# Threshold attention and hash-routed experts on one core: PSUM tiles at the seam, and the order of gathers and weight loads

## The chip, the core and the metric

The kernel runs on one NeuronCore of a Trainium2 chip. The metric is the time of one execution on the device in microseconds (us), lower is better; the median of several runs counts. Five engines work side by side, each with its own instruction queue, and wait for each other through semaphores: PE (TensorE, with weight loads shown as PEld), DVE (VectorE), ACT (ScalarE), POOL (GpSimd) and SP (SyncE, which here only issues transfers).

## The reference, cut to what matters

Attention over 8 batches of 8 heads (576 queries, 64 wide) keeps only scores within `tau` of the row's maximum. Its output is seen as 4608 rows of 512, and each row goes to one of 8 experts by a hash of its token id:

```python
scores = scale * np.matmul(q, k.transpose(0, 1, 3, 2))
thresh = np.max(scores, axis=-1, keepdims=True) - tau
scores = np.where(scores >= thresh, scores, -1000000000.0)
...
attn = attn / (np.sum(attn, axis=-1, keepdims=True) + 1e-09)
out = np.matmul(attn, v)
...
expert_idx = token_ids * np.int64(2654435761) % np.int64(E)
for e in range(E):
    xe = x[mask]
    h = np.maximum(xe @ w1[e], 0.0)
    out[mask] = h @ w2[e]
```

`w1[e]` is 512 x 1024 and `w2[e]` is 1024 x 512, all in fp32. A weight load is 2 MB.

## The kernel before

The attention half walks over 32 pairs of heads in 5 steps each, in an order written out by hand (`tc.manual_schedule()`): queues execute instructions as the source emits them. Scores are made in PSUM tiles `sc` of the pool `ps_sc` (two tiles of two banks each, line 87). [...]

The experts' half runs over the experts e = 0 to 7 in an order sorted by load. Each expert has two layers, and each layer is computed with seven products in place of eight (a Strassen scheme, function `seven`, line 930): sums and differences of blocks of weights and inputs are made on VectorE (`left` and `right`, line 862 for subtractions, line 865 for additions), PE multiplies them (line 945), and the results are added up from PSUM on VectorE. `layer1` runs `seven` twice for each expert (a product of layer 2 is 16 matmul rows in the trace, one of layer 1 is 8), `layer2` once. After each of a product's results, `seven` calls back a "side" function with a step number 0 to 5; side work of other experts is emitted there: `side1` in layer 1, `side2` in layer 2.

At the seam, expert 0's first layer has been started while attention was still running (`early_h`, line 641: three quarters of the contraction, blocks fo 0 to 7). `late_h` (line 661) adds the last quarter. It takes the blocks in the order 0, 6, 1, 7, 2, 3, 4, 5; blocks 6 and 7 were held open in `ps_sc`'s two tiles, blocks 2 and 4 use these two tiles next, and blocks 0, 1, 3 and 5 use the pool `ps_x`, which has one tile. For all but 6 and 7 VectorE adds the PSUM tile to h (line 672) and ScalarE applies the relu (line 673). Then `ps_sc` is closed (line 1079) and a pool `ps_m` of four tiles opens over the same PSUM (line 1080); `bank2` (line 858) hands out its tiles for all products that follow.

The work of an expert that matters here:

- `fetch(e)` (line 1048) gathers expert e's rows of x into the five tiles `xg` by five indirect DMAs on POOL's queue (line 122). For e = 1 each has a small copy ahead of it (line 1052) that makes it wait for a relu of `late_h`.
- `turn_x(e)` (line 1055): VectorE transposes the five tiles into `xq` (line 1059), then SP issues 16 DMAs, the moves, that lay them out as `xT` (line 1067).
- `load_w1` and `load_w2` (lines 135 and 141) load weights on SP's queue (DMAs of lines 137 and 143) into pools of two tiles; each reads the expert's number into a register first (line 132). `load_w1(e + 2)` must wait for expert e's layer 1.
- `sums_w1(e + 1)` and `sums_x(e + 1)` are emitted two at a time in steps 1 to 5 of layer 2 of expert e; the sums over x need the moves.
- `put_squares` transposes results on VectorE (line 1031) and scatters them with indirect DMAs on POOL's queue (line 1039).

For expert 0 all of `turn_x(1)` runs in step 0 of layer 2. For the later experts it runs within layer 1 of the expert before.

Of the kernel before, what the change touches and what calls it, by code (L numbers as in the profile page):

```python
# [9 lines left out]
FP32 = mybir.dt.float32  # L10
# [6 lines left out]
PSUM = bass.MemoryType.PSUM  # L17
# [3 lines left out]
def kernel(  # L21
# [16 lines left out]
    E, _, F = w1.shape  # L38
    P = 128
# [43 lines left out]

    consts = ctx.enter_context(tc.tile_pool(name="consts", bufs=1))
    w_pool = ctx.enter_context(tc.tile_pool(name="w_pool", bufs=2))
    sc_stack = ctx.enter_context(ExitStack())
    ps_sc = sc_stack.enter_context(tc.tile_pool(name="ps_sc", bufs=2, space=PSUM))

    ident = consts.tile([P, P], FP32, name="ident")
    u128 = consts.tile([P, P], BF16, name="u128")  # L90
# [30 lines left out]
    def gather(src, dst, idx):  # L121
        nc.gpsimd.indirect_dma_start(  # L122
            out=dst, out_offset=None, in_=src,
            in_offset=bass.IndirectOffsetOnAxis(ap=idx, axis=0),
            bounds_check=src.shape[0] - 1, oob_is_err=False)
# [4 lines left out]
    def expert_at(e):  # L130

        return nc.values_load(order_i[0:1, e:e + 1], engines=[mybir.EngineType.SP],
                              min_val=0, max_val=E - 1)

    def load_w1(e):
        w1_sb = w_pool.tile([P, CO, F], FP32, name="w1_sb")
        nc.sync.dma_start(out=w1_sb[:],
                          in_=w1[bass.ds(expert_at(e), 1)].rearrange("o (c p) f -> p (o c) f", p=P))
        w_tiles[e, 1] = w1_sb
# [7 lines left out]
    with tc.tile_pool(name="a_q", bufs=1) as a_q, \  # L147
# [513 lines left out]
        def late_h(new_tile):  # L661

            w1_sb = w_tiles.pop((0, 1))
            for fo in LATE:
                h_ps = held.pop(fo) if fo in held else new_tile(fo)
                for i in range(2):
                    nc.tensor.matmul(h_ps[:, i, 0:CH0], lhsT=w1_sb[:, CO - 1, fo * P:fo * P + P],
                                     rhs=xT_0[:, CO - 1, i * CH0:i * CH0 + CH0],
                                     start=(fo < FO - 2), stop=True)
                h3 = h_0[:, fo, 0:caps[0]].rearrange("p (i t) -> p i t", i=2)  # L670
                if fo < FO - 2:
                    nc.vector.tensor_tensor(out=h3, in0=h3, in1=h_ps[:, :, 0:CH0], op=ALU.add)
                    nc.scalar.activation(h3, h3, AF.Relu)
                else:
                    nc.scalar.activation(h3, h_ps[:, :, 0:CH0], AF.Relu)
# [17 lines left out]
        def fill(n):  # L693
            for _ in range(n):
                next(h_pieces, None)
# [140 lines left out]
    with tc.tile_pool(name="m_x", bufs=1) as m_x, \  # L836
# [18 lines left out]
        halves = [m_s.tile([P, 2, CH], FP32, name=n) for n in ("p1", "u2", "u3", "u4")]  # L855
        CHL = 32 * (NB - 4) // 2

        def bank2():
            return ps_m[0].tile([P, 2, 512], FP32, name="bank2")

        def sub(out, in0, in1):
            return lambda: nc.vector.tensor_tensor(out=out, in0=in0, in1=in1, op=ALU.subtract)  # L862
# [47 lines left out]
        def sums_w1(e):  # L910
            return left(*w1_blocks(w_tiles[e, 1]), triple(w1_s, 0, C2))

        def sums_w2(e):
            s1 = None
            if e == E - 1:
                spare = w_pool.tile([P, CO, F], FP32, name="w1_sb")
                s1 = w_tiles["s1"] = spare[:, :, 0:D2]
            return left(*w2_blocks(e, w_tiles[e, 2]), w2_sums(e), s1)

        def sums_x(e):  # L920
            return right(*x_blocks(e), triple(x_s, 0, C2, caps[e] // 2))

        def sums_h(e, c0, c1):
            return right(*h_blocks(c0, c1, half2(e)), triple(h_s, c0, c1, half2(e)))

        def run(work, n=1):
            for _ in range(min(n, len(work))):
                work.pop(0)()
# [38 lines left out]
        def layer1(e, side):  # L967

            w, half = w_tiles.pop((e, 1)), caps[e] // 2
            for g in range(NG):  # L970
                outs = [h_0[:, FH * i + 2 * g:FH * i + 2 * g + 2, half * k:half * k + half]
                        for i in range(2) for k in range(2)]
                seven(w1_blocks(w), triple(w1_s, 0, C2), x_blocks(e), triple(x_s, 0, C2, half), 2 * P * g,
                      outs, True, lambda step: side(g, step))

        def layer2(e, side):

            w, half = w_tiles[e, 2], half2(e)
            outs = [oT[:, C2 * i:C2 * i + C2, half * k:half * k + half]
                    for i in range(2) for k in range(2)]  # L980
            a = w2_blocks(e, w)
            if e == E - 1:
                a[2] = w_tiles["s1"]
            seven(a, w2_sums(e), h_blocks(0, FH, half),
                  triple(h_s, 0, FH, half), 0, outs, False, side)
# [42 lines left out]
        def put_squares(e, i):  # L1028

            s0, s1 = ((0, NH), (NH, -(-caps[e] // 32)))[i]  # L1030
            nc.vector.transpose(  # L1031
                out=o_q[i][:, 0:s1 - s0].rearrange("p n a c -> p c n a"),
                in_=oT[:, :, 32 * s0:32 * s1].rearrange("p c (n q) -> p c n q", q=32))
            for s in range(s0, s1):
                put_rows(o_q[i][:, s - s0].rearrange("p a c -> p (a c)"), qidx[:, e, s:s + 1],
                         rows=out_q)
# [11 lines left out]
        def fetch(e):  # L1048
            for k in range(KT):
                if e == 1:  # L1050

                    nc.gpsimd.tensor_copy(mark[0:1, :], h_0[0:1, k, 0:1])
                gather(x_dram, xg_bufs[k][:], gidx_x[:, e, k:k + 1])

        def turn_x(e):


            def squares(k):
                return lambda: nc.vector.transpose(
                    out=xq[:, :, 32 * k:32 * k + 32],  # L1060
                    in_=xg_bufs[k][:].rearrange("p (d a) -> p d a", a=32))

            def move():
                for g in range(4):
                    s0, s1 = 32 * KT * g, min(32 * KT * (g + 1), caps[e])
                    for r in range(4):
                        nc.sync.dma_start(out=xT_bufs[e % 2][32 * r:32 * r + 32, :, s0:s1],  # L1067
                                          in_=xq[32 * g:32 * g + 32, r::4, 0:s1 - s0])

            return [squares(k) for k in range(KT)] + [move]  # L1070

        with tc.tile_pool(name="ps_x", bufs=1, space=PSUM) as ps_x, tc.manual_schedule():
            run(sums_w2(0), 4)
            fill(18)
            late_h(lambda fo: (ps_sc.tile([P, 2, 512], FP32, name="sc") if fo in (2, 4) else
                               ps_x.tile([P, 2, 512], FP32, name="xT_ps")))
            fetch(1)
            run(sums_h(0, 0, FH), 4)
        sc_stack.close()
        ps_m = [ctx.enter_context(tc.tile_pool(name="ps_m", bufs=4, space=PSUM))]  # L1080

        with tc.manual_schedule():
            for e in range(E):
                more = e + 1 < E
                turns = turn_x(e + 1) if more else []

                if e > 0:
                    w2_work, h_work = sums_w2(e), sums_h(e, 0, 2)

                    def side1(g, step):  # L1090
                        if g == 0:
                            run(w2_work)
                            if step == 0:
                                put_squares(e - 1, 1)
                        else:
                            run(h_work)
                        if step > 2:
                            run(turns, 1 if g == 0 else 2)

                    layer1(e, side1)  # L1100
                    run(sums_h(e, 2, FH), 4)
                if e + 2 < E:
                    load_w1(e + 2)
                x_work = (sums_w1(e + 1) + sums_x(e + 1)) if more else []

                def side2(step):
                    if step == 0:
                        run(turns, len(turns))
                        if e + 2 < E:
                            fetch(e + 2)  # L1110
                    else:
                        run(x_work, 2)
                    if more and step == 3:
                        put_squares(e, 0)
                    if not more and step == 4:
                        put_out(e, (0,))

                layer2(e, side2)
                run(x_work, len(x_work))
                if e + 2 < E:  # L1120
                    load_w2(e + 2)


            def middle():
                put_out(E - 1, (1, 2), (3,))

            last_tile(middle)
# [74 lines left out]
```

## Time and profile before

| what | value |
|---|---|
| median of 3 runs | 922.66 us (922.28 to 922.70) |
| the profiled execution | 933.93 us |
| span of its trace | 932.2 us |
| granted TensorE clock, mean | 0.998 |
| bytes moved by DMA | 113.11 MB, mean 121 GB/s |
| PE, stage 0 to 528 us | 517.94 us busy |
| PE, stage 900 to 933 us | 25.12 us busy |

The profiled execution is 1.2% longer than the median of the plain runs. Its span leaves out 1.7 us around the program. Times within it are counted from the start of the span. In a line of the timeline the columns are start, length, engine, source line, operation, output and inputs by the program's names, shape, and the count of merged instructions; brackets hold the idle time of the engine before it and what ended that. SPq lines are DMAs that SyncE issues; their length is the time of issuing, not of the transfer.

### The profile page before, as it was taken

The numbers are of one execution on the slowest core, as the hardware profiler recorded it, in microseconds if no ns is written. First come the engines' busy times: TensorE is split into PE (matmuls) and PEld (weight loads), VectorE is DVE, ScalarE is ACT, GpSimd is POOL, SyncE is SP. The second block draws the span as 40 slices with busy tenths as digits, with TensorE's granted clock in tenths as the row PEclk, the third lists the DMA queues.
The fourth block names the chain that finished last, engine by engine and source line by source line (L and its number), as shares of the span: only waits on it lengthen the run. The fifth ranks groups of instructions, "written<-read, shape, count | busy, mean of one in ns | idle before, by whom it ended". The sixth has DMA issues, their size and how long they took to land.

```text
span 932.2 us, 20728 instructions
## 1 busy us (share of the span) xinstructions
PE 911.4 (98%) x7495; PEld 662.9 (71%) x7495; DVE 759.5 (81%) x1658; ACT 458.3 (49%) x741; POOL 408.1 (44%) x522
## 2 busy tenths in 40 slices
PE   7999999999999999999999998999999999999996
PEld 4666666666666666665667877888887978879785
DVE  7999999999999999999854685867867686786741
ACT  6888888888888889888702010110202112020210
POOL 4233332436666653465323371643717164350712
PEclk9999999999999999999999999999999999999999
DMA  7355454463555666852113616355352734511101
GB/s 179 88 146 124 107 147 108 120 151 92 115 129 168 151 172 178 211 127 64 32 25 140 191 54 186 126 124 192 93 173 100 196 127 121 200 43 44 46 8 54
DMA packets 114807, 113.11 MB, mean 121 GB/s; under 512 B 32456, under 2 KB 89318, under 8 KB 114704
## 3 DMA queue, kind: packets, MB, share of 16 engines
q1 hardware_dynamic: 105168, 92.64, 37.2%
q0 software_dynamic: 9104, 18.91, 7.2%
q8 instruction: 61, 1.00, 0.4%
q14 instruction: 42, 0.34, 0.1%
q10 hardware_dynamic: 432, 0.21, 0.1%
HBM read 81.99 MB, written 21.50 MB: 111 GB/s over the span
## 4 chain that ended last, share of the span: by engine, by line
PE 62%; issue 21%; POOL 8%; DVE 3%; DMA 2%; ACT 2%; another core or an unknown queue 1%; SPq 1%; POOLq 0%; DVEq 0%; ACTq 0%
PE av L316 18%; PE sc L238 15%; PE bank L945 13%; PE tr L285 11%; POOL out_dram L1039 6%; PE sc L649 3%; PE av L285 1%; POOL xg L122 1%; DMA xT<-xq 1%; ACT w L263 1%; DMA xg<-x_scratch,gidx_x 1%; DMA k_sb<-in_k_dram 1%; ACT wT_b L306 1%; SPq L1067 0%
## 5 line engine op out<-in xcount | busy, mean ns | idle before, releaser
L263 ACT ACTIVATE w<-ns,nmx 128x576 f32<-128x576 f32 x288 | 220.4, 777 | 28.5 <-DVE ns L249 28.2
L1039 POOL DMA_INDIRECT out_dram<-o_q,qidx x128 | 141.0, 1102 | 194.8 <-DVE o_q L1031 133.8
L274 DVE SCALAR_TENSOR_TENSOR w<-ns,thr,w 128x576 f32<-128x576 f32 x288 | 226.2, 817 | 0.0
L249 DVE TENSOR_SCALAR_CACHE_REDUCE ns<-sc 128x576 f32<-128x576 f32 x288 | 205.7, 747 | 7.6 <-PE sc L238 6.6
L256 POOL TENSOR_SCALAR thr<-nmx,drop 128x2 f32<-128x2 f32 (+1 forms) x160 | 104.5, 653 | 186.7 <-DVE ns L249 174.1
L238 PE MATMUL sc<-k_sb,q 64*128 64x288 f32 (+1 forms) x1280 | 178.6, 423 | 0.9 <-DVE ns L249 0.5
L285 PEld LDWEIGHTS tr<-ident,w 64*128 64x128 f32 x2624 | 106.1, 138 | 94.6 <-ACT wT_b L306 32.7
L285 PE MATMUL tr<-ident,w 64*128 64x64 f32 x2624 | 139.0, 230 | 6.1 <-ACT wT_b L306 2.8
L952 ACT ACTIVATE h<-h 128x576 f32<-128x576 f32 (+1 forms) x56 | 38.8, 693 | 158.8 <-DVE h L865 127.8
L238 PEld LDWEIGHTS sc<-k_sb,q 64*128 64x128 f32 (+1 forms) x1280 | 92.8, 177 | 23.2 <-DVE ns L249 8.5
L955 ACT COPY p<-bank 128x576 f32<-128x576 f32 (+2 forms) x22 | 14.0, 635 | 183.4 <-PE bank L945 157.9
L316 PE MATMUL av<-wT_a,v 128*64 128x320 f32 (+1 forms) x704 | 100.4, 418 | 0.4 <-DVE xm L355 0.3
L945 PE MATMUL bank<-h,w_sb 128*128 128x288 f32 (+2 forms) x384 | 95.6, 405 | 2.3 <-issue 1.5
L945 PEld LDWEIGHTS bank<-h,w_sb 128*128 128x128 f32 x384 | 92.5, 294 | 4.2 <-issue 1.9
L306 ACT COPY wT_a<-tr 128x512 f32<-128x512 f32 (+1 forms) x128 | 81.7, 638 | 20.7 <-PE tr L285 20.2
L306 ACT COPY wT_b<-tr 128x512 f32<-128x512 f32 (+1 forms) x128 | 81.4, 636 | 15.3 <-PE tr L285 8.6
L945 PE MATMUL bank<-xT,w_sb 128*128 128x288 f32 (+1 forms) x336 | 87.5, 410 | 0.0
L316 PE MATMUL av<-wT_b,v 128*64 128x256 f32 x640 | 83.2, 389 | 0.0
L945 PEld LDWEIGHTS bank<-xT,w_sb 128*128 128x128 f32 x336 | 63.8, 190 | 19.0
L945 PE MATMUL bank<-h_s,w_s 128*128 128x288 f32 (+2 forms) x256 | 63.0, 404 | 1.9 <-DVE h_s L862 1.9
L316 PEld LDWEIGHTS av<-wT_a,v 128*64 128x64 f32 x704 | 43.7, 136 | 29.2 <-DVE xm L355 0.8
L945 PEld LDWEIGHTS bank<-h_s,w_s 128*128 128x128 f32 x256 | 50.0, 195 | 13.3 <-DVE h_s L862 2.3
(168 smaller groups left out, 1117.7 us busy)
## 6 DMA issues: line engine op xcount, KB each, us to landing
w_sb<-in_moe_w_dram SPq DMA_DIRECT2D x16, 2048.0 KB
q<-in_q_dram SPq DMA_DIRECT2D x62, 288.0 KB
v<-in_v_dram SPq DMA_DIRECT2D x32, 256.0 KB
x_scratch<-xm SPq DMA_DIRECT2D x32, 256.0 KB
xT<-xq SPq DMA_DIRECT2D x84, 80.0 KB
k_sb<-in_k_dram SPq DMA_DIRECT2D x31, 144.0 KB
k_sb<-in_k_dram SPq DMA_DIRECT2D x32, 112.0 KB
x_scratch<-xg SPq DMA_DIRECT2D x9, 256.0 KB
```

What stands on the lines that cost most here:

```text
L238: nc.tensor.matmul(sc[out_rows, i, 0:S2], lhsT=q_sb[rows, h, q0:q1], rhs=k_sb[rows, h], start=True, stop=True)
L249: nc.vector.tensor_scalar(out=ns[:].rearrange("p (i s) -> p i s", i=2), in0=sc[:, :, 0:S2], scalar1=-1.0, scalar2=None, op0=ALU.mult, op1= ...
L256: nc.gpsimd.tensor_scalar(out=thr[:, 0:j + 1], in0=stats[n][0][:, 0:j + 1], scalar1=drop[:], scalar2=None, op0=ALU.add)
L263: nc.scalar.activation(w, nss[n, j][:], AF.Exp, bias=stats[n][0][:, j:j + 1], scale=-1.0)
L274: nc.vector.scalar_tensor_tensor(out=w, in0=nss.pop((n, j))[:], scalar=stats[n][1][:, j:j + 1], in1=w, op0=ALU.is_le, op1=ALU.mult, accum_ ...
L285: nc.tensor.transpose(dst[:, r, 64 * c:64 * c + 64], src[rows, c0:c0 + P], ident[rows, rows])
L306: nc.scalar.copy(dst, tr[:, :, 0:64 * n_c].rearrange("p r (c q) -> p r c q", c=n_c))
L316: nc.tensor.matmul(av[64 * j:64 * j + 64, g, c0:c1], lhsT=v_sb[:, c, 64 * j:64 * j + 64], rhs=wT[g][:, i, c0:c1], start=(c == 0), stop=stop)
L649: nc.tensor.matmul(h_ps[:, i, 0:CH0], lhsT=w1_sb[:, co, fo * P:fo * P + P], rhs=xT_0[:, co, i * CH0:i * CH0 + CH0], start=(co == 0), stop= ...
L945: nc.tensor.matmul(ps[:, i, 0:width], lhsT=lhsT, rhs=y[:, c], start=c == 0, stop=c == n_k - 1)
L952: nc.scalar.activation(c, c, AF.Relu)
L1039: inst = nc.gpsimd.indirect_dma_start(out=rows[:, :], out_offset=bass.IndirectOffsetOnAxis(ap=idx, axis=0), in_=o_sb, in_offset=None, boun ...
```

## The change

`ps_sc` stays open to the end. The pools `ps_x` and the four-tile `ps_m` give way to one `ps_m` of two tiles, opened before `late_h`, which takes from it what it took from `ps_x`. `bank2` hands out tiles of the two pools in turn. In `side2`, `fetch(e + 2)` moves from step 0 to step 2, and `load_w1(e + 2)` from ahead of layer 2 to step 4.

```diff
-    sc_stack = ctx.enter_context(ExitStack())
-    ps_sc = sc_stack.enter_context(tc.tile_pool(name="ps_sc", bufs=2, space=PSUM))
+    ps_sc = ctx.enter_context(tc.tile_pool(name="ps_sc", bufs=2, space=PSUM))
...
+        ps_m = ctx.enter_context(tc.tile_pool(name="ps_m", bufs=2, space=PSUM))
+        turn = [0]
+
         def bank2():
-            return ps_m[0].tile([P, 2, 512], FP32, name="bank2")
+            turn[0] ^= 1
+            if turn[0]:
+                return ps_sc.tile([P, 2, 512], FP32, name="sc")
+            return ps_m.tile([P, 2, 512], FP32, name="bank2")
...
-        with tc.tile_pool(name="ps_x", bufs=1, space=PSUM) as ps_x, tc.manual_schedule():
+        with tc.manual_schedule():
             run(sums_w2(0), 4)
             fill(18)
             late_h(lambda fo: (ps_sc.tile([P, 2, 512], FP32, name="sc") if fo in (2, 4) else
-                               ps_x.tile([P, 2, 512], FP32, name="xT_ps")))
+                               ps_m.tile([P, 2, 512], FP32, name="bank2")))
             fetch(1)
             run(sums_h(0, 0, FH), 4)
-        sc_stack.close()
-        ps_m = [ctx.enter_context(tc.tile_pool(name="ps_m", bufs=4, space=PSUM))]
...
-                if e + 2 < E:
-                    load_w1(e + 2)
                 x_work = (sums_w1(e + 1) + sums_x(e + 1)) if more else []
 
                 def side2(step):
                     if step == 0:
                         run(turns, len(turns))
-                        if e + 2 < E:
-                            fetch(e + 2)
                     else:
                         run(x_work, 2)
+                    if step == 2 and e + 2 < E:
+                        fetch(e + 2)
+                    if step == 4 and e + 2 < E:
+                        load_w1(e + 2)
```

## The prediction

> **What bounds the kernel now.** I read the page first, then busy time by stage, then the instructions in order of time around the seam between attention and experts, then SyncE's queue. The page says who the bound is:
>
> ```profile
> span 932.2 us, 20728 instructions
> ...
> PE 911.4 (98%) x7495; PEld 662.9 (71%) x7495; DVE 759.5 (81%) x1658; ACT 458.3 (49%) x741; POOL 408.1 (44%) x522
> ```
>
> TensorE is busy for 98% of the span, so only its gaps can be won. Busy time by stage, for the experts' half (columns: stage length; busy of PE, PEld, DVE, ACT, POOL; clock; DMA share; GB/s):
>
> ```profile
> 528.00:545.00 17.00, 16.64 (x70) 12.80 (x69) 16.02 (x17) 2.01 (x3) 9.65 (x9) 1.00 0.45 155
> 545.00:575.00 30.00, 26.68 (x108) 22.14 (x107) 17.68 (x27) 5.16 (x8) 15.24 (x15) 1.00 0.54 148
> 575.00:600.00 25.00, 25.00 (x104) 21.41 (x103) 19.58 (x21) 1.32 (x2) 10.76 (x10) 1.00 0.39 135
> ...
> 640.00:900.00 260.00, 260.00 (x1056) 216.28 (x1055) 187.88 (x225) 36.93 (x55) 117.11 (x107) 1.00 0.38 113
> ```
>
> From 575 to 900 PE never stops. So whatever PE gains before 575 reaches the end undiminished, and buffers or loads cannot give anything later. Gaps exist at three places: the seam, one at 534, one near 565 to 571. The seam in order of time (start, length, engine, line; the idle time before it in brackets):
>
> ```profile
> 493.78 1.13 PE L667 MATMUL xT_ps<-xT,w_sb 128*128 128x288 f32 x4
> 494.75 1.13 PE L667 MATMUL sc<-xT,w_sb 128*128 128x288 f32 x4
> 495.82 0.78 PEld L667 LDWEIGHTS xT_ps<-xT,w_sb 128*128 128x128 f32 x4 [0.40 <-DVE h L672]
> ...
> 500.82 1.24 PE L667 MATMUL xT_ps<-xT,w_sb 128*128 128x288 f32 x4
> ...
> 502.10 0.75 DVE L672 TENSOR_TENSOR h<-h,xT_ps 128x576 f32<-128x576 f32 x1 [0.36 <-PE xT_ps L667]
> ...
> 502.90 8.15 PE L945 MATMUL bank<-h,w_sb 128*128 128x288 f32 x32 [0.84 <-DVE h L672]
> 503.60 1.36 DVE L862 TENSOR_TENSOR h_s<-h 128x1152 f32<-128x1152 f32 x1 [0.75 <-ACT h L673]
> ...
> 511.84 3.07 DVE L1059 STREAM_TRANSPOSE xq<-xg 128x512 f32<-128x512 f32 x5
> ...
> 616.51 7.92 PE L945 MATMUL bank<-h,w_sb 128*128 128x288 f32 x32
> ```
>
> The last line is the same product pair two experts on, for comparison. The reader is to see two things. late_h's blocks on the single xT_ps tile wait for VectorE's add of the block before. And expert 0's first product (502.90) waits for the last of these adds (502.10 + 0.75 = 502.85), although it reads only h blocks 0 to 3: the sum over block 5 is none of its operands. It is the pools that make this wait, ps_m's four tiles opening over ps_sc and ps_x only when both are free. SyncE's queue at the same place, and the next gap:
>
> ```profile
> 502.09 0.39 SPq L137 DMA_DIRECT2D w_sb<-in_moe_w_dram  x1
> 514.97 12.52 SPq L1067 DMA_DIRECT2D xT<-xq  x16
> 528.35 0.41 SPq L143 DMA_DIRECT2D w_sb<-in_moe_w_dram  x1
> ...
> 528.91 0.76 DVE L862 TENSOR_TENSOR x_s<-xT 128x576 f32<-128x576 f32 x1 [5.42 <-DMA xT<-xq]
> ...
> 534.70 4.12 PE L945 MATMUL bank<-x_s,w_s 128*128 128x288 f32 x16 [0.36 <-DVE x_s L862]
> ```
>
> The 16 moves that turn x for expert 1 land at 528.9; VectorE waits 5.42 us for them, and PE for its sums: the 16 rows from 530.29 should end at 534.17, the next start at 534.70, a gap of 0.5 us.
>
> [...] In this trace the w2 load issued at 528.35 follows the moves and they still land by 528.9. [...] In this trace PE is full from 575 to 900 with loads of 2 MB in flight.
>
> **The change part by part.**
>
> *late_h on two tiles.* No instruction is added. An unhindered block of four rows takes 494.75 - 493.78 = 0.97 us. Eight blocks from 493.78 end at 493.78 + 8 x 0.97 = 501.54. Blocks 1, 3, 5 now wait for the add two turns earlier (0, 1), done by 497.85: no wait. Blocks 2 and 4 still wait for ScalarE's relu of the held blocks 6 and 7, which by the same timeline end at 497.02 and 499.11; their turns come at 493.78 + 4 x 0.97 = 497.66 and 493.78 + 6 x 0.97 = 499.60. Covered, by 0.5 us.
>
> *First product.* Its bank is now that of block 2, whose add ends at 499.04 + 0.75 = 499.79. It reads blocks 0 to 3; the relu of block 3 ends at 500.80 + 0.68 = 501.48. So it starts at 501.54 instead of 502.90: 1.36 us. Its 32 rows took 8.15 us against 7.92 at 616.51, because the row after the wait comes late: 0.23 us. Sum 1.59 us.
>
> *What is late next.* Product 2 starts at 501.54 + 3.88 = 505.42 (16 rows, 3.88 us apart by the products at 632.03 and 635.91) and reads block 5, whose relu ended at 503.56. Product 3 needs the third of the h_s sums: it ended at 507.74, and comes about 0.3 us earlier as block 5 ends at 501.54 instead of 501.82; needed at 509.30. Slack 1.9 us, before 3.1. Not late. Bounds for this part: the waits gone cannot give more than all idle of PE at the seam, 1.6 us; if the product met another wait of the same pools it would be the add of block 5 again, about 0.3 us earlier than now: 0.3 us gained. I take 1.59.
>
> *The rotation of banks.* bank2 alternates ps_sc and ps_m, two tiles each: still four in turn. Each product of the experts waits for the same instruction as before, by the built order of both kernels. Cost 0.
>
> *Gathers two products later.* In GpSimd's queue nothing stands between the old place and the new one, and each gather waits, as before, for the VectorE transpose that read its xg tile. All five issue where they did. The words of the change describe the source, not the queue. Cost 0; cover is not needed.
>
> *w1 loads four products later.* For experts 3 to 7 SyncE's queue has the same order as before (the moves were issued in layer 1 already), so nothing moves. For expert 2's w1 the DMA and its expert number (a register load and three small instructions) go past the 16 moves: from 502.09 to behind them, before w2's load. First use: the sums at 574.71, which wait for it. Two loads now run together after about 527; 4 MB, at the 385 GB/s that the slice at 532 shows for one, take about 11 us, so about 540, doubled for caution 550. Cover 25 us. What leaves 502 to 511 is the load that ran beside expert 1's gathers; their transposes (511.84) showed no idle time, so nothing is won there. What joins 527 to 540 is beside GpSimd's scatters, which stand 1.3 to 1.5 us apart under a load (534.25, 535.73, 537.01) and 1.3 without one (546.45, 547.74). Cost 0, bounds -0.5 (the gap at 534 goes) to +0.3 (the last moves are touched).
>
> *The end.* put_out's two tiles wait for copies long done. 0.
>
> The moves start when the five transposes are done, and these follow the first oT add, which follows product 2. So the moves, their landing and the gap at 534 all come 1.59 us earlier, and PE keeps what it won. The profiled execution took 933.93 us (span 932.2); it becomes 932.3. The median of the runs is 922.66, 1.2% lower; the waits are engine latencies, which I don't scale: 922.66 - 1.6 = 921.1 us, -0.17%. (0.2%, about what a measurement can tell from no change, is 1.85 us here.)
>
> **The rivals.**
>
> *More than the seam* (919): the DMA side changes with the load gone from the gathers' time, and the gap at 534 (0.5) and part of the stall near 565 to 571 go. The stage 545 to 575 lacks 30.00 - 26.68 = 3.3 us of PE. Half of that and 0.5 beyond the seam's 1.6: 922.66 - 1.6 - 0.5 - 1.6 = 919.0. For: the stall lies where moves and gathers crowd the DMA engines. Against: no weight load lies there, before or after.
>
> *Taken back at 534* (922.7): the moves land at the old time, because their own transfers set it, and PE waits 1.6 us longer. For: that wait is live, so nothing buffers it. Against: the moves' start is tied to product 2.
>
> *Slower* (929): the w1 load, issued right behind the 16th move, gets on the DMA engines before the last moves have landed. The live wait for x_s passes each microsecond on to PE. The load took from 502.09 to about 511, over 8 us; all of it ahead of the moves gives 922.66 - 1.6 + 8 = 929.1. It decides from a delay of 1.6 + 1.85 = 3.45 us. Against: the w2 load already stood at that place, 0.86 us behind the last move (514.97 + 12.52 = 527.49 to 528.35), and did no harm.
>
> *It doesn't do what it says* holds for the gathers and for all w1 loads but one, and is in the sum.
>
> **How the numbers follow.** Seam alone 0.60, more 0.20, taken back 0.08, slower 0.12. Around 1.6 us the seam alone falls beyond 1.85 us in somewhat under half its cases (0.27), because the waits in timed runs may be a little longer and the small gap at 534 may shrink. Faster 0.27 + 0.20 = 0.47; same 0.33 + 0.08 = 0.41; slower 0.12. The time is 921.1. The range, 918.4 to 923.0, leaves out the slower case and the far end of "more".
>
> **What would show it.** Right: L667's blocks 0.97 us apart without idle; the first L950 row at about 501.5 in the changed kernel, its 32 rows in 7.9 us; x_s still waiting some 5 us for xT; the w1 load at about 527, just ahead of w2's; gathers right after the transposes; PE full after 575. Wrong: a wait for VectorE at the first product; x_s's wait grown by over a microsecond; idle PE at the sums of w1 near 574; a different gap near 565 that outweighs the seam.

## The result, and the profile after

| | median | range | executions |
|---|---|---|---|
| before, beside it on the same chip | 922.62 us | 921.77 to 923.83 | 22 |
| after | 921.12 us | 920.38 to 922.09 | 22 |

The ratio is 0.9984, with a 95% interval of 0.9978 to 0.9990: 1.5 us faster (0.9 to 2.0 by the interval). That is clear of zero in these 22 executions of each, but below the 0.2% (1.85 us) that the prediction took as the least that counts as faster. The predicted time was 921.1 us.

The page of the kernel after:

```profile
span 919.5 us, 20728 instructions
...
PE 906.9 (99%) x7495; PEld 662.5 (72%) x7495; DVE 758.2 (82%) x1658; ACT 457.6 (50%) x741; POOL 408.9 (44%) x522
```

Its span is 12.7 us below the one shown of before, and the medians are 1.5 us apart. So most of what these two profiles differ by is not the change. The waits of PE show it. Each line has what PE was to compute and the line of the source, what it waited for, and then us in total, the number of waits and the longest; "issue" is a wait for nothing that the profile shows. Before:

```profile
PE tr L285 <- ACT wT_b L306: 2.8, 4, 1.7
...
PE bank L945 <- DVE h_s L862: 1.9, 1, 1.9
...
PE bank L945 <- issue: 1.5, 2, 1.0
PE bank L945 <- DVE h L672: 0.8, 1, 0.8
...
PE bank L945 <- DVE x_s L862: 0.4, 1, 0.4
```

After, the whole view:

```profile
PE tr L284 <- ACT wT_a L305: 2.0, 3, 0.7
PE tr L701 <- POOL ident masks.py:199: 1.6, 1, 1.6
PE av L315 <- DVE xm L354: 0.3, 1, 0.3
PE sc L237 <- DVE drop L712: 0.3, 1, 0.3
PE av L284 <- ACT oT L331: 0.2, 1, 0.2
PE sc L237 <- DVE ns L248: 0.2, 1, 0.2
```

No wait of the experts' products (L945 before, L950 after) is left. Only one of the four that went, the 0.8 us for h, is the seam's. The line of `tr` and `wT_b` stands in the attention half, where both kernels hold the same instructions: late_h's first block starts at 487.20 us after and at 493.78 before, and these 6.58 us come from that half alone. From that block to the end of the span it is 432.3 us (919.5 - 487.2) against 438.4 (932.2 - 493.8), 6.1 us. What of this belongs to the change is read against late_h's first block. The timeline of after at the seam:

```profile
487.20 1.13 PE L666 MATMUL bank<-xT,w_sb 128*128 128x288 f32 x4
488.17 1.13 PE L666 MATMUL sc<-xT,w_sb 128*128 128x288 f32 x4
...
493.99 1.13 PE L666 MATMUL bank<-xT,w_sb 128*128 128x288 f32 x4
494.96 4.04 PE L950 MATMUL sc<-h,w_sb 128*128 128x288 f32 x16
495.16 0.75 DVE L671 TENSOR_TENSOR h<-h,bank 128x576 f32<-128x576 f32 x1 [0.22 <-PE bank L666]
...
499.45 1.36 DVE L867 TENSOR_TENSOR h_s<-h 128x1152 f32<-128x1152 f32 x1
502.72 4.04 PE L950 MATMUL sc<-h_s,w_s 128*128 128x288 f32 x16
...
504.64 1.00 POOL L121 DMA_INDIRECT xg<-x_scratch,gidx_x  x1 [4.32 <-DVE xq L1064]
506.88 10.88 SPq L1072 DMA_DIRECT2D xT<-xq  x16
```

Blocks of four rows follow each other by 0.97 us, and the first product (494.96) starts before the add of block 5 (495.16), with no idle time in front of it: 7.76 us after late_h's first row (494.96 - 487.20), against 9.12 before (502.90 - 493.78). Then SyncE's queue, and the product that needs the moved x:

```profile
518.63 0.42 SPq L136 DMA_DIRECT2D w_sb<-in_moe_w_dram  x1
519.25 0.76 DVE L867 TENSOR_TENSOR x_s<-xT 128x576 f32<-128x576 f32 x1 [3.93 <-DMA xT<-xq]
519.88 0.39 SPq L142 DMA_DIRECT2D w_sb<-in_moe_w_dram  x1
522.12 2.10 PE L950 MATMUL bank<-xT,w_sb 128*128 128x288 f32 x8
...
526.00 2.10 PE L950 MATMUL bank<-x_s,w_s 128*128 128x288 f32 x8
```

The w1 load at 518.63 now stands behind the 16 moves (506.88 + 10.88 = 517.76) and ahead of w2's. VectorE waits 3.93 us for the moves, and PE doesn't: its rows at 522.12 and 526.00 are 16 rows, 3.88 us, apart. Expert 1's first product starts at 522.12, 34.92 us after late_h's first row; before, it started at 530.29, which is 36.51 us after it. The seam's part is the difference, 1.59 us. In windows (length; busy PE, PEld, DVE, ACT, POOL, each with its count of instructions; clock; DMA share; GB/s) PE is full from there on:

```profile
529.00:559.00 30.00, 30.00 (x126) 25.23 (x125) 23.16 (x31) 5.96 (x9) 20.72 (x20) 1.00 0.48 138
559.00:584.00 25.00, 25.00 (x105) 21.52 (x104) 17.43 (x18) 1.32 (x2) 8.30 (x8) 1.00 0.59 198
624.00:884.00 260.00, 260.00 (x1053) 216.42 (x1053) 189.48 (x226) 36.35 (x54) 116.31 (x107) 1.00 0.37 113
```

So of the 6.1 us, 1.59 lie at the seam, some 0.6 at the gap that was at 534, and most of the rest in the stage where before showed 26.68 busy us of 30.00. Whether the change removed that stall too was the first question for the runs, since that would have been the rival *more than the seam*.

### The profile page after: what moved, and what is told of

Same layout as the page of the kernel before. It is cut to its first block, busy times and chain, and to the rows that moved or that the text cites. A ratio compares the mean times of both kernels' runs of the same rounds, so it can differ in the third digit from the quotient of the medians.

```text
span 919.5 us, 20728 instructions
## 1 busy us (share of the span) xinstructions
PE 906.9 (99%) x7495; PEld 662.5 (72%) x7495; DVE 758.2 (82%) x1658; ACT 457.6 (50%) x741; POOL 408.9 (44%) x522
## 4 chain that ended last, share of the span: by engine, by line
PE 73%; issue 16%; POOL 5%; DMA 3%; ACT 2%; DVE 1%; POOLq 0%; SPq 0%; DVEq 0%; ACTq 0%
PE av L315 18%; PE sc L237 16%; PE sc L950 12%; PE bank L950 11%; PE tr L284 11%; POOL out_dram L1044 4%; PE sc L648 3%; DMA out_dram<-o_q,qidx 2%; PE av L284 2%; POOL xg L121 1%; ACT w L262 1%; PE bank L666 0%; PE sc L666 0%; DVE ns L248 0%; DMA k_sb<-in_k_dram 0%
## 5 line engine op out<-in xcount | busy, mean ns | idle before, releaser
L960 ACT COPY p<-bank 128x576 f32<-128x576 f32 (+2 forms) x11 | 7.0, 634 | 108.6 <-PE bank L950 84.1
L315 PEld LDWEIGHTS av<-wT_b,v 128*64 128x64 f32 x640 | 40.2, 136 | 18.8 <-issue 0.8
L550 POOL DMA_INDIRECT slot_scratch<-tok,slot_i x36 | 47.9, 1330 | 10.4 <-issue 6.9
L960 ACT COPY p<-sc 128x576 f32<-128x576 f32 (+1 forms) x11 | 7.0, 640 | 84.7 <-PE sc L950 84.7
L950 PE MATMUL bank<-h,w_sb 128*128 128x288 f32 (+2 forms) x192 | 48.4, 405 | 0.0
L950 PE MATMUL sc<-h,w_sb 128*128 128x288 f32 (+2 forms) x192 | 47.7, 402 | 0.0
L950 PEld LDWEIGHTS bank<-h,w_sb 128*128 128x128 f32 x192 | 46.9, 298 | 0.5
```

What stands on the lines that cost most here:

```text
L315: nc.tensor.matmul(av[64 * j:64 * j + 64, g, c0:c1], lhsT=v_sb[:, c, 64 * j:64 * j + 64], rhs=wT[g][:, i, c0:c1], start=(c == 0), stop=stop)
L550: nc.gpsimd.indirect_dma_start(out=slot_dram[c % 2][:, :], out_offset=bass.IndirectOffsetOnAxis(ap=slot_i[:, c:c + 1], axis=0), in_=tok[:, ...
L950: nc.tensor.matmul(ps[:, i, 0:width], lhsT=lhsT, rhs=y[:, c], start=c == 0, stop=c == n_k - 1)
```

## Experiments

Two theories. *Seam*: the gain is made by the PSUM pools alone, 1.6 us, and the moved transfers do nothing. *Transfers*: the gain, or the part of it after the seam, comes from gathers and loads that moved. The runs were made on four chips, here named A to D. The kernel before took 942.29 us on A, 922.53 on B, 942.62 on C and 922.72 on D; its executions lay 11.6 us apart on A and 10.1 us on C, 1.8 us on B and 2.3 us on D. Each ratio is to the kernel before on the same chip.

| run | chip | what is changed | median us | ratio | 95% interval |
|---|---|---|---|---|---|
| e1_pools | A | pools alone | 940.36 | 0.9976 | 0.9959 to 0.9992 |
| e2_loads | A | gathers and loads alone | 941.15 | 0.9988 | 0.9970 to 1.0005 |
| e3_gathers | A | gathers alone | 941.90 | 0.9998 | 0.9979 to 1.0017 |
| e5_two_tiles | A | second tile for late_h alone | 942.10 | 0.9997 | 0.9978 to 1.0017 |
| e4_load_in_moves | B | after, w1 load among the moves | 929.14 | 1.0076 | 1.0059 to 1.0093 |
| e6_twice | B | after, 24 more rows in late_h | 927.03 | 1.0052 | 1.0035 to 1.0068 |
| r1_after | C | the kernel after | 942.47 | 0.9994 | 0.9974 to 1.0013 |
| r2_pools | C | pools alone | 941.27 | 0.9979 | 0.9956 to 1.0001 |
| r3_loads | C | gathers and loads alone | 944.12 | 1.0033 | 1.0014 to 1.0053 |
| r4_two_tiles | C | second tile for late_h alone | 943.18 | 1.0010 | 0.9992 to 1.0028 |
| q1_pools | D | pools alone | 920.93 | 0.9979 | 0.9970 to 0.9989 |
| q2_loads | D | gathers and loads alone | 922.61 | 0.9998 | 0.9990 to 1.0006 |

### The pools alone

The runs e1_pools, r2_pools and q1_pools are the kernel after, with gathers and w1 load put back to where before has them:

```diff
                     run(sums_h(e, 2, FH), 4)
+                if e + 2 < E:
+                    load_w1(e + 2)
...
                         run(turns, len(turns))
+                        if e + 2 < E:
+                            fetch(e + 2)
                     else:
                         run(x_work, 2)
-                    if step == 2 and e + 2 < E:
-                        fetch(e + 2)
-                    if step == 4 and e + 2 < E:
-                        load_w1(e + 2)
```

> The pools' part alone: ps_sc stays open and bank2 takes turns, but gathers stay in step 0 and w1's load ahead of layer 2. Seam theory (all of the gain is the wait at the first product and late_h's waits): the whole gain, 1.5 us less than before, ratio about 0.9984; in the profile the first product directly behind late_h's eighth block, 7.76 us after the first block's start. Transfers theory (the gain is expert 2's w1 load leaving the time of expert 1's gathers): no gain, ratio 1.000, or at most 0.3 us.

> The pools' part alone again, since the first chip scattered by 1% and left room for both theories. Seam theory: the same as the changed kernel beside it, ratio about 0.9984. Transfers theory: at least 1 us slower than the changed kernel, ratio 0.9995 or more.

> The pools' part alone a third time, in the hope of a chip that scatters less (the first two took 942 us for the kernel before and scattered by 1%). Seam theory: 1.4 to 1.7 us less than before, ratio 0.9982 to 0.9985. Transfers theory: under 0.5 us less.

Chip D can tell it: 920.93 us, 0.9979 (0.9970 to 0.9989), no less than the whole change gives. That is 1.8 us (1.0 to 2.8 by the interval), a little more than the 1.4 to 1.7 expected. The intervals of A and C hold the ratio of the whole change too, but C's also holds 1. The timeline of q1_pools:

```profile
486.76 1.13 PE L666 MATMUL bank<-xT,w_sb 128*128 128x288 f32 x4
...
493.55 1.13 PE L666 MATMUL bank<-xT,w_sb 128*128 128x288 f32 x4
494.52 4.04 PE L950 MATMUL sc<-h,w_sb 128*128 128x288 f32 x16
...
494.71 0.39 SPq L136 DMA_DIRECT2D w_sb<-in_moe_w_dram  x1
...
506.36 11.91 SPq L1072 DMA_DIRECT2D xT<-xq  x16
```

The first product is again 7.76 us behind late_h's first row, with the w1 load (494.71) still ahead of the moves. The gain does not need the moved load. In all six profiles with the new pools and no rows added to late_h (after, e1, e4, r1, r2, q1), A to D among their chips, the distance is 7.76 us. In the five with the old pools and one tile (before, e2, e3, r3, q2) it is 9.12 or 9.13.

### Gathers and loads alone

The runs e2_loads, r3_loads and q2_loads are the kernel before, with the lines of `side2` as the change has them and its own pools:

```diff
-                if e + 2 < E:
-                    load_w1(e + 2)
...
                         run(turns, len(turns))
-                        if e + 2 < E:
-                            fetch(e + 2)
                     else:
                         run(x_work, 2)
+                    if step == 2 and e + 2 < E:
+                        fetch(e + 2)
+                    if step == 4 and e + 2 < E:
+                        load_w1(e + 2)
```

> The other part alone: pools as before, gathers in step 2 and w1's load in step 4. Seam theory: no change, ratio 1.000 within 0.0005; the first product still waits for the add of block 5, about 9.1 us after late_h's first block. Transfers theory: 1 to 1.5 us less, ratio about 0.9985, and no gap at the sums over x of expert 1.

> Gathers and loads alone again, for the same reason. Seam theory: ratio 1.000 within 0.0005. Transfers theory: 0.9985.

> Gathers and loads alone a third time, beside it. Seam theory: no change, 1.000 within 0.0005, first product 9.13 us after late_h's first block as before. Transfers theory: 1 to 1.5 us less, 0.9985.

On D 922.61 us, 0.9998 (0.9990 to 1.0006): nothing, and the interval leaves no room for 1.6 us. On A nothing either. On C the interval (1.0014 to 1.0053) lies above 1. I don't count this as a cost of the loads: it is the same kernel, and A and D contradict it, D with executions of it within 1.9 us (922.13 to 923.99) where on C they spread over 12.5 us. But the other pair on C leans the same way, the moved transfers with the new pools (r1_after, 942.47) against the new pools alone (r2_pools, 941.27), so a cost that only such a chip shows isn't excluded. Why C gave it stays open. The timeline of q2_loads:

```profile
496.38 0.75 DVE L672 TENSOR_TENSOR h<-h,xT_ps 128x576 f32<-128x576 f32 x1 [0.36 <-PE xT_ps L667]
...
497.19 8.15 PE L945 MATMUL bank<-h,w_sb 128*128 128x288 f32 x32 [0.84 <-DVE h L672]
```

The wait at the first product is that of the kernel before to the hundredth, 0.84 us, and 8.15 us for the 32 rows. Later in the same kernel:

```profile
522.58 0.42 SPq L137 DMA_DIRECT2D w_sb<-in_moe_w_dram  x1
523.18 0.76 DVE L862 TENSOR_TENSOR x_s<-xT 128x576 f32<-128x576 f32 x1 [5.41 <-DMA xT<-xq]
...
528.97 4.12 PE L945 MATMUL bank<-x_s,w_s 128*128 128x288 f32 x16 [0.35 <-DVE x_s L862]
```

The wait for the moves is 5.41 us where before had 5.42, so the w1 load issued behind the moves (522.58) doesn't delay them. It could hardly: x_s starts at 523.18, 0.6 us after it. The gap at this product comes and goes between executions: about 0.5 us in before, q2, r3 and r4, none in e2 and e3, which also have the old pools, 0.36 in e1 and none in q1, which are the same kernel. The traces show what it goes with. In all profiles but e4's, VectorE's wait for the moves lies between 3.93 us (after) and 5.44 (r4), and the gap is what exceeds 4.9 us of it: 5.42 leaves 0.53 in before, 5.26 leaves 0.36 in e1, and 4.84 leaves nothing in e3. So a gain here is a matter of how long the moves take in the one execution.

On chip D, from late_h's first row to the end of the span it is 432.3 us in q1 (919.1 - 486.76), as in after, and 434.3 in q2 (922.4 - 488.06). These 2.0 us are the 1.59 of the seam and some 0.5 of this gap.

### Gathers alone

The run e3_gathers is the kernel before with only the gathers moved:

```diff
                         run(turns, len(turns))
-                        if e + 2 < E:
-                            fetch(e + 2)
                     else:
                         run(x_work, 2)
+                    if step == 2 and e + 2 < E:
+                        fetch(e + 2)
```

> Only the gathers in step 2, all else as before. GpSimd's queue and its waits are then the same as before, so this kernel is also the kernel before once more. Both theories: no change, ratio 1.000 within 0.0005. Its profile tells whether the stall of 4 us after the second product of expert 1's layer 2 and the 6.6 us that the profile of before needed more up to late_h belong to the kernel or to that one execution: if to the kernel they are here again; I expect them gone or different.

0.9998 (0.9979 to 1.0017), which leaves about 2 us each way, the scatter of chip A. The trace says more: the first gather that waits for a transpose starts 19.03 us behind late_h's first row (513.29 - 494.26), in before too (512.81 - 493.78). The gathers don't move.

The other expectation was wrong. Both things that were to be "gone or different" are there: late_h starts at 494.26, as late as in before, and the stall after the second product of layer 2 is there with waits of 0.91, 0.77 and 1.62 us. The section on the stall comes back to both.

### A second tile for late_h alone

Two things change at the seam: late_h gets a second tile, and pools are no longer closed and reopened. The runs e5_two_tiles and r4_two_tiles have the first without the second, on the kernel before:

```diff
-        with tc.tile_pool(name="ps_x", bufs=1, space=PSUM) as ps_x, tc.manual_schedule():
+        with tc.tile_pool(name="ps_x", bufs=2, space=PSUM) as ps_x, tc.manual_schedule():
```

> The kernel before with two tiles in ps_x in place of one; the pools are still closed and reopened before the first product. Splits the seam. If the reopening is what costs (seam theory in its narrow form): late_h's waits go, about 0.3 us by the profile of before, the first product still waits for the add of block 5, and 1.1 to 1.3 us of the gain are missing: ratio about 0.9997. If the single tile is what costs: the whole gain, 0.9984.

> The kernel before with two tiles in ps_x again, for the same reason. If the reopening of pools costs: about 0.3 us gained, ratio 0.9997. If the single tile costs: 0.9984.

The times (0.9997 and 1.0010, intervals about 0.2% each way) can't tell a third of a microsecond. The timeline of e5_two_tiles can:

```profile
494.05 1.13 PE L667 MATMUL xT_ps<-xT,w_sb 128*128 128x288 f32 x4
...
500.84 1.13 PE L667 MATMUL xT_ps<-xT,w_sb 128*128 128x288 f32 x4
...
502.01 0.76 DVE L672 TENSOR_TENSOR h<-h,xT_ps 128x576 f32<-128x576 f32 x1 [0.22 <-PE xT_ps L667]
```

late_h's eight blocks are 0.97 us apart here too, so its own waits are gone (500.84 - 494.05 = 7 x 0.97). Yet the first product waits for block 5's add, which ends at 502.77: it starts at 502.82, 8.77 us behind late_h's first row, and so it does in r4_two_tiles. Before had 9.12, after has 7.76. Expert 1's first product comes 36.15 us behind that row, against 36.51 in before and 34.92 in after. Of the 1.59 us the second tile is worth 0.36 and the pools that stay open 1.23.

A rival is that the product's tile just happens to lie over block 5's tile. The programs as built rule it out. The first tile of `ps_m` lies in PSUM banks 0 and 1, which were block 2's; block 5's tile lies in banks 4 and 5 in before, and in 6 and 7 with two tiles in `ps_x`. In both, the product's first matmul waits on the semaphore count of block 5's add. With the pools left open, it lies in banks 0 and 1 again and waits for block 2's add only.

### Is a microsecond at the seam a microsecond at the end?

The run e6_twice is the kernel after, with the matmuls of six of late_h's blocks issued twice, the second time over the first: 24 rows more, 24 x 0.2425 = 5.8 us.

```diff
-                for i in range(2):
+                for i in (0, 1, 0, 1) if fo < FO - 2 else (0, 1):
```

> The changed kernel, with late_h's two matmuls of blocks 0 to 5 done twice into the same tile (the second time overwrites the first): 6 x 0.97 = 5.8 us more of PE at the seam. If what PE wins or loses at the seam reaches the end in full: 5.8 us more than the changed kernel, about 926.9. If transfers set the time behind the seam (the moves for expert 1 land at their own time): part of it is swallowed, under 4 us more.

```profile
486.90 2.10 PE L666 MATMUL bank<-xT,w_sb 128*128 128x288 f32 x8
...
500.48 1.86 PE L950 MATMUL sc<-h,w_sb 128*128 128x288 f32 x7
```

In this timeline the first product stands 13.58 us behind late_h's first row, 5.82 more than in after. From late_h's first row to the end of the span it is 438.3 us (925.2 - 486.90), 6.0 more than in after. The median of its 4 executions is 927.03, 5.9 us over the 921.12 of after, measured in other runs. Against the kernel before on chip B it is 4.5 us more (3.2 to 6.3 by the interval), where 5.8 - 1.5 = 4.3 were due, and under 2.5 if part had been swallowed. Time at the seam reaches the end in full.

### The slower rival, made to happen

The run e4_load_in_moves is the kernel after, with expert 2's w1 load issued between the 8th and the 9th of the 16 moves:

```diff
+                    if e == 1 and g == 1:
+                        load_w1(2)
...
-                    if step == 4 and e + 2 < E:
+                    if step == 4 and 0 < e < E - 2:
                         load_w1(e + 2)
```

> The changed kernel, with expert 2's w1 load between the eighth and the ninth of the 16 moves of expert 1. This makes the slower rival's accident on purpose. If the load delays the moves behind it as that rival priced it: the last moves land up to 8 us later, VectorE's wait for xT grows from 3.9 us to 8 or more, PE stops at the products over sums of x, and the time grows by 3 to 7 us against the changed kernel, so 924 to 928. If the moves pass beside the load: within 0.5 us of 921.1.

929.14 us in 4 executions, 6.6 over the kernel before beside it: above the 924 to 928 expected. The timeline:

```profile
507.07 5.61 SPq L1072 DMA_DIRECT2D xT<-xq  x8
...
513.74 0.42 SPq L136 DMA_DIRECT2D w_sb<-in_moe_w_dram  x1
...
524.24 2.10 PE L950 MATMUL sc<-xT,w_sb 128*128 128x288 f32 x8
524.76 0.76 DVE L867 TENSOR_TENSOR x_s<-xT 128x576 f32<-128x576 f32 x1 [9.25 <-DMA xT<-xq]
...
530.48 4.18 PE L950 MATMUL bank<-x_s,w_s 128*128 128x288 f32 x8 [4.13 <-DVE x_s L867]
```

late_h starts at 487.38 in this execution, so x_s starts 37.38 us behind it, in after 32.05 (519.25 - 487.20): the moves land 5.3 us later. The product starts at 43.10 instead of 38.80 us, 4.3 later, since 1.0 us of slack lay between. And then its eight rows take 4.18 us instead of 2.10. The windows of this kernel show the clock:

```profile
526.40:530.40 4.00, 0.00 (x0) 0.00 (x0) 3.97 (x5) 0.00 (x0) 1.39 (x2) 0.80 0.98 344
530.40:534.70 4.30, 4.22 (x9) 3.11 (x10) 4.30 (x5) 0.68 (x1) 3.43 (x3) 0.50 0.47 176
534.70:540.00 5.30, 5.30 (x21) 4.07 (x21) 5.30 (x7) 0.02 (x1) 4.34 (x4) 0.91 0.16 51
```

The mean granted clock (third number from the end; 1.00 is full speed) is 0.80 in the window in which PE waits, 0.50 in the 4.30 us from 530.40, where it starts again (530.48) after 4.13 us of waiting, and 0.91 in the 5.30 us after that. By the same timeline the next rows start at 534.45 and 536.99, so these 16 rows took 6.51 us instead of 3.88: 2.6 more. The wait and the slow rows, 4.3 + 2.6 = 6.9 us, nearly make up the 7.1 us between the two profiled executions (928.21 and 921.14). The medians, from different runs, lie 8.0 us apart.

### The stall near 565 to 571

The run r1_after is the kernel after again, unchanged, on C.

> The changed kernel again, beside the next three on one chip. Both theories: ratio 0.9984, as before.

Its time there, 0.9994 (0.9974 to 1.0013), tells nothing about 0.16%. But its timeline has the stall that the first profile of the kernel after lacks ("remote" is an end of a wait that the profile puts down to nothing on this core):

```profile
563.72 0.40 PE L950 MATMUL sc<-h,w_sb 128*128 128x288 f32 x1 [1.21 <-issue]
...
565.12 1.62 PE L950 MATMUL sc<-h,w_sb 128*128 128x288 f32 x6 [1.00 <-issue]
565.20 0.76 DVE L870 TENSOR_TENSOR h<-sc,u 128x576 f32<-128x576 f32 x1 [4.10 <-remote]
```

It is there in every profile of A and C, with new pools and with old, and in none of B and D, new pools (e4, e6, q1) or old (q2). So the stall goes with the chip or the execution, not with the pools, gathers or loads. The late start of late_h goes the same way: 493.4 to 496.6 us in every profile of A and C, as in the profile of before, and 486.8 to 488.1 on B and D, as in that of after. This settles the rest of the 6.1 us, and the 6.58 us ahead of late_h: they are not the change's. On A and C more time is lost later in the experts' half, in kernels of both kinds: from the first layer-2 product over h_s and w_sb after 560 us to the end of the span it is 363.8 us in r1_after (939.8 - 576.01) and 365.2 in e2_loads (944.3 - 579.08), against 354.7 in q1_pools (919.1 - 564.36) and 354.6 in q2_loads (922.4 - 567.84). What causes the stalls wasn't found, and no run here tried it.

## Why the prediction was right

*late_h on two tiles and the first product.* Foreseen 1.36 us to the first product's start and 1.59 with its rows: measured 1.36 and 1.59. The reading of the pools as the cause was the step that mattered. e5 confirms it: with late_h's waits gone, the reopened pools still hold the product until block 5's add, and 1.23 of the 1.59 us are theirs. One reading was too broad. Not every block on the single tile waits for the add of the block before. Blocks 1 and 5 do, and block 3 doesn't: it starts at 498.84, two blocks of 0.97 us behind block 7 (496.90).

*Late next.* The third h_s sum ends at 499.45 + 1.36 = 500.81 and is needed at 502.72: 1.9 us of slack, as worked out.

*Gathers.* Cost 0, right. The first that waits for a transpose starts 17.44 us behind late_h's first row (504.64 - 487.20) in after and 17.43 (504.19 - 486.76) in q1, which has the gathers in step 0.

*w1 loads.* One load moved, from ahead of the moves to behind them, at no cost on D: q2's interval allows 0.6 us. Placed 33.2 us behind late_h's first row (527), it came at 31.4, because the moves were issued in 10.88 us instead of 12.52.

*The gap at 534.* Said to come 1.59 us earlier and stay. In after it isn't there, and it also comes and goes in pairs of runs of one kernel. The prediction took one execution's wait of 5.42 us as fixed. It lies so close to the 4.9 us from which on PE stops that the quicker moves of another execution remove the gap.

*The end.* That what PE gains reaches the end undiminished was read from a stage of 260 busy us in 260, and e6 shows it with 5.9 of 5.8 us. The 1.6 us weren't scaled to the faster runs, and these gave 1.5. That 921.1 met 921.12 so closely is luck: the interval of the gain is 0.9 to 2.0 us.

*The rivals.* More than the seam (0.20): the profile alone would have spoken for it, but the median gained 1.5 us and the pools alone give that, and r1_after shows the stall in the kernel after. This rival is why faster had a little more chance than same, 0.47 to 0.41, and there the larger chance was put on the wrong side: 0.16% lies just inside the 0.2%, where the prediction put most of the cases of the seam alone. What the rival counted on was a stall that belongs to the profiled execution. Taken back at 534: the moves started 1.5 us earlier after late_h's first row (19.68 against 21.19) and landed earlier. Slower: its place in SyncE's queue was right, and so, by chance, was its price of 929.1. The step that priced it was not: it put 8 us down to the transfer alone, and in e4 the moves landed 5.3 us later, 1.0 of it absorbed, and 2.6 us were slow rows of TensorE (granted clock 0.50 from 530.40 to 534.70), which the sum didn't have. It didn't occur in the kernel after because the load stands behind the last move, not among them.

## What to carry to other kernels

A PSUM pool that is closed and reopened between two stages can be a barrier: the first tile of the new pool waits for the last reader of the old ones, though the data don't ask for it. Here that wait was 0.84 us in before and 0.85 in e5_two_tiles, and the reopened pools were 1.23 of the seam's 1.59 us. Keep the pools open across the seam, and look at which instruction the first product waits for, and whether that made one of its operands or last used its tile. For gains of a fifth of a per cent measure distances from a fixed instruction within the traces, and take part of the change on a chip whose runs lie close together, before believing the difference of two profiles.

## What the runs showed of the hardware

The kernel before took 922.5 to 922.7 us in three sets of runs (beside the first result, on B and on D) and 942.3 to 942.6 us on A and C, where its executions also lay 10 to 12 us apart. The seam doesn't differ: with the new pools the first product comes 7.76 us behind late_h's first row on all of them.

Slow rows also followed shorter waits than the 4.13 us of e4. In the stall PE waited 1.00, 0.51 and 1.87 us in e2_loads and 0.95, 0.50 and 1.86 us in before, almost the same, and only e2_loads slowed down: the 28 rows behind the last wait took 8.76 us there (from 570.48) and 7.07 in before (from 570.81). The windows of e2_loads show a lower granted clock in them:

```profile
570.00:572.00 2.00, 1.52 (x6) 1.21 (x7) 1.86 (x3) 0.00 (x0) 0.00 (x0) 0.93 0.79 231
572.00:576.00 4.00, 4.00 (x12) 2.92 (x11) 0.60 (x1) 0.00 (x0) 0.00 (x0) 0.61 1.00 401
```

and those of before keep 1.00:

```profile
569.00:571.00 2.00, 0.19 (x1) 0.19 (x2) 1.90 (x4) 0.00 (x0) 0.00 (x0) 1.00 0.44 59
571.00:575.00 4.00, 4.00 (x17) 3.26 (x17) 2.18 (x4) 0.00 (x0) 0.00 (x0) 1.00 0.95 346
```

Two more kernels have slow rows at this place: six rows from 567.23 took 2.59 us in r2_pools, where six took 1.62 in r1_after (from 565.12), and five from 567.31 took 2.77 us in r3_loads, where five took 1.38 in e3_gathers (from 566.71). The waits just before them were 1.02 us in r2_pools and 0.33 in r3_loads. What decides whether slow rows follow a wait was not shown.
